# One piece of w1 and w2 under way at a time, the modulation's columns in two parts, and six attention steps ahead of the MLP

## The chip, the cores and the metric

The kernel runs on one core of a Trainium2 chip. Its time is the device time of one execution in microseconds. A core has a matrix engine (TensorE, PE in the profile), three engines for elementwise work (VectorE or DVE, ScalarE or ACT, GpSimd or POOL) and SyncE (SP), which here issues nearly all transfers; the transfers of all queues run on the core's 16 DMA engines. Each engine works its instructions off in the order in which they stand in the program, and waits for others by semaphores.

## The reference

The input is x of 2048 tokens with 448 columns, and everything is bfloat16. The block is an attention with a sliding dilated window and an MLP, both with a layer norm modulated by a condition c:

```python
mod = (_silu(c) @ w_mod).reshape(c.shape[0], 6, 1, -1)     # sa, ca, ga, sb, cb, gb
h = _layernorm(x) * (1 + ca) + sa
x = x + ga * A(h, wqkv, wo)      # 16 heads of 28; each token sees 8 tokens, two apart, itself and those before
h = _layernorm(x) * (1 + cb) + sb
x = x + gb * B(h, w1, b1, w2, b2)   # layer norm, gelu(y @ w1 + b1) @ w2 + b2, with 1792 inner columns
```

## The kernel before

The tokens are taken as two halves, the even and the odd ones, so that the dilated window becomes a window of 8 neighbours. There are 16 blocks of 128 tokens. The work is cut into named pieces ("items"), and a small planner (`Plan.schedule`) places them: it gives each item an engine and a start by a table of assumed durations, with a priority that is made of the length of the chain behind the item, a bias for its kind, its place in the sequence of tokens, and a correction of its own (`delta`). The program is then written out in the order of the planned starts, and the hardware keeps that order on each engine. Nothing is planned while the kernel runs.

The items in the order of the data:

- `ldwmod1` loads three pieces of w_mod (rows 0 to 255 and 320 to 447 in two, and the 64 rows from 256 in the third). `modcol` (L497 to L503) multiplies silu(c) with it, 8 columns of 4 parts each, and `mcol` makes of it the scale and shift of the first norm.
- `st`, `pw`, `nm`, `zt`, `md` are the first norm, the turning of its result (on TensorE for the first eight blocks, L559; by a DMA transpose for the others, L551) and the modulation into `hT`.
- `qk` multiplies `hT` with `Wqk`, in five chunks of tokens; `v` multiplies it with `Wv`. V goes to a DRAM buffer `vd` (`vt`, L693) and comes back as `vb` (`vl`, L759), laid out by windows. `wcp` (copies at L296 and L298) builds `Wqk` from the raw weights.
- `attention(d)` is one of nine steps of four windows each, 57 tokens per window: `lt` (logits, L726), `ex` (exponential, L736), `mk` (mask, L743), `dn` (row sums, L770), `pv` (L783), `ln` and `rc` (the reciprocal of the sums by logarithm and exponential, L793, L798), `on` (normalisation into `qT`, L807).
- `wo_pair` multiplies with wo and adds to x (L824, L833). `norm2` is the second and the third norm, on VectorE and GpSimd, and ends with a DMA transpose into `hT` (L890).
- `w1_pairs(q)` and `w2_block(b)` are the MLP of a quarter of the tokens: seven pairs of multiplications with w1 (L619 and L626 with tile `w`), gelu (L917), and four blocks of fourteen multiplications with w2 (L933), whose rows are scaled by gb beforehand (`w2s`, L1010). The last block is cut in two column parts (L940).
- `fill` are multiplications of zeros (L465), 28 of them, which the planner puts where TensorE would have nothing else at the start.

`CFG['phases']` sets the order of attention steps (E) and MLP quarters (G). ScalarE's exponentials and gelus need different tables, so the ScalarE work of a phase waits for that of the phase before; the multiplications with w1 wait for the logits of the phase before, those with w2 for nothing of the kind:

```python
CFG['phases'] = [['E', [0, 1, 2, 3, 4]], ['G', [0]], ['E', [5, 6, 7, 8]], ['G', [1, 2, 3]]]
```

The loads are items too. With `lag=n` a load waits for the landing of the load n places ahead of it. The wait is on SyncE, so all transfers that stand behind it in SyncE's order wait with it. The w1 and w2 loads (L577 to L587, four pieces each of 336 or 448 KB) have `lag=3`, and are held until the eight DMA transposes of the first norm have landed. The planner counts for a load 1.1 us from its start, its bytes at 0.36 MB per us, and a landing time; for the `vl` loads the landing time is 1.0.

Of the kernel before, what the change touches and what calls it, by code (L numbers as in the profile page):

```python
# [14 lines left out]
S, D, H, DH, F = 2048, 448, 16, 28, 1792  # L15
NB = S // 128
SL = S // 2
OFF = [0, 128, 192, 320]
# [19 lines left out]
    "nfill": 26,  # L38
    "gq": 1,
# [27 lines left out]
class Plan:  # L67
# [162 lines left out]
CFG["tail"], CFG["slope"], CFG["window"] = 0.0735, 17.2213, 0.15  # L230
CFG["bias"] = {
    "bce": (-107.09, 0.452),
    "cst": (91.44, 8.357),
    "dn": (-20.05, 0.02),
    "exp": (-542.16, 2.185),
    "gelu": (-247.7, 0.104),
    "h2": (-372.66, 40.0),
    "ln": (-71.79, 0.407),
    "lt": (349.79, 5.389),
    "md": (250.29, 14.017),  # L240
    "mk": (378.46, 0.25),
    "mod2": (-102.92, 0.065),
    "nm1": (-212.52, 0.208),
    "nm2": (420.37, 6.471),
    "on": (253.1, 18.885),
    "out": (363.15, 37.438),
    "pow1": (586.93, 0.02),
    "pow2": (49.28, 7.0),
    "pv": (-143.36, 3.574),
    "qk": (-468.53, 40.0),  # L250
    "qke": (-147.02, 0.024),
    "rc": (-599.49, 0.048),
    "st1": (-127.6, 15.441),
    "st2": (244.63, 15.735),
    "store": (143.43, 0.039),
    "v": (487.87, 3.471),
    "ve": (-355.16, 0.031),
    "vl": (-306.46, 8.681),
    "vt": (-492.77, 0.115),
    "w1": (37.08, 26.927),  # L260
    "w2": (-223.49, 40.0),
    "w2s": (-535.94, 19.732),
    "wcp": (-165.13, 0.443),
    "wo": (147.83, 14.91),
    "wos": (433.82, 16.205),
    "x1": (-329.74, 0.192),
    "xp": (-205.62, 0.972),
    "yt": (-95.58, 0.094),
    "zt": (-495.74, 2.221),
    "ztp": (-35.54, 0.05),  # L270
}
CFG['phases'] = [['E', [0, 1, 2, 3, 4]], ['G', [0]], ['E', [5, 6, 7, 8]], ['G', [1, 2, 3]]]
# [13 lines left out]
def build_plan(cfg):  # L286
    P = Plan(cfg)
    T = Names()
    add, val = P.add, P.val
# [13 lines left out]
    def psf(v):  # L303
        return T.ps[v.slot]
# [45 lines left out]
    def fn(e):  # L350
        memset(e, T.nhalf[:], -0.5)
# [9 lines left out]
    woz = add("woz", "cst", {"ACT": 1.7}, fn, rd=["zero"], wr=["woz"])  # L361
# [128 lines left out]
    def fn(e):  # L490
        copy(e, T.silu_bc[:], T.silu[:].unsqueeze(2).to_broadcast([128, 4, 32]))
    add("silubc", "mod2", {"DVE": 0.2, "ACT": 0.3}, fn, rd=["silu"], wr=["silu_bc"])

    v2 = val("ps", "modcol")

    def fn(e):
        w = wmod1()  # L497
        for g in range(8):
            vv, j = divmod(g, 4)
            for kt in range(4):  # L500
                T.nc.tensor.matmul(psf(v2)[:, g:g + 1], lhsT=w[:, kt, vv * D + OFF[j]:vv * D + OFF[j] + 128],
                                   rhs=T.silu[:, kt:kt + 1], start=(kt == 0), stop=(kt == 3))
    add("modcol", "front", {"PE": 0.9}, fn, rd=[("wmod1", 0), ("wmod1", 1), ("wmod1", 2), "wmodz", "silu"], wr=["ps_mod"], vals=[v2, fv])  # L503

    def fn(e):
        T.nc.vector.tensor_tensor(out=T.mcol[:], in0=psf(v2)[:, 0:8], in1=T.oz[:], op=ALU.add)
    add("mcol", "front", {"DVE": 0.1}, fn, rd=["ps_mod", "oz"], wr=["mcol"], vals=[v2])


    for m in range(4):  # L510
        for a in range(2):
            def fn(e, a=a, m=m):
                c0 = a * 512 + m * 128
                dst = T.Wqk[:, :, c0:c0 + 128].rearrange("p s (h e) -> p s h e", e=32)[:, :, :, 0:DH]
                c0 = a * D + m * 112
# [61 lines left out]
    for hh in range(2):  # L577
        for j in range(2):
            def fn(e, hh=hh, j=j):
                return e.dma_start(**overl(T.w1[:, :, 896 * hh:896 * hh + 896], T.w1_d, j, 896 * hh, 896 * hh + 896))  # L580
            load(f"ldw1{hh}{j}", 256 * 896 * 2, fn, [("w1", hh, j)], lag=3, hold=zts)
    W2P = [(0, 4), (4, 7), (7, 11), (11, 14)]
    for i, (f0, f1) in enumerate(W2P):
        def fn(e, f0=f0, f1=f1):
            return e.dma_start(out=T.w2[:, f0:f1, :],
                               in_=T.w2_d.rearrange("(ft p) n -> p ft n", p=128)[:, f0:f1, :])
        load(f"ldw2{i}", (f1 - f0) * 128 * 896, fn, [("w2", f) for f in range(f0, f1)], lag=3, hold=zts)  # L587
# [120 lines left out]
    def attention(d):  # L708
# [44 lines left out]
        for u in range(2):  # L753
            k0 = sub_tok(4 * d + 2 * u) - (WIN - 1)

            def fn(e, u=u, k0=k0):
                src = bass.AP(tensor=T.vd.tensor, offset=T.vd.offset + (16 + k0) * D,
                              ap=[[D, SK], [SQ * D, 2], [1, D]])
                T.nc.sync.dma_start(out=T.vb[vbv.slot][64 * u:64 * u + 64, :, 0:D], in_=src)  # L759
            add(f"vl{d}.{u}", "vl", {"SP": 0.6}, fn, rd=[("vd", b // 2) for b in blocks_of(k0, SQ + SK)] + ["ebuf", "vdz"],  # L760
                wr=[("vb", d, u)], vals=[vbv], land=(1.0, 128 * 896))
# [410 lines left out]
```

## Time and profile before

| what | value |
|---|---|
| median of 3 runs | 178.07 us (176.08 to 178.91) |
| the profiled execution | 177.01 us |
| its span | 175.3 us |
| granted TensorE clock | 0.999 |
| TensorE busy | 165.8 us, 95% of the span |
| VectorE, ScalarE, GpSimd busy | 117.6, 108.9, 38.8 us |
| read from and written to HBM | 11.87 and 3.70 MB |

The profile is one execution, seen by the hardware's profiler. A row of a group gives the line, the engine, the operation, what it writes and reads, how many there were, and then the busy time, the mean duration in ns, and the idle time of the engine just before, with what ended it. "issue" stands for an idle time that nothing in the profile ended. In the timeline a row begins with its start and its duration in us. The rows of stages give for each stretch the time, then busy time and number of instructions for PE, PEld (the weight loads of TensorE), DVE, ACT and POOL, the granted clock, the share of the DMA engines that was busy and the rate.

### The profile page before, as it was taken

How to read it: one execution, taken by the hardware profiler on the slowest of the kernel's cores; microseconds unless marked ns; L12 is line 12 of the kernel's file. 1: busy time of each engine (PE TensorE's matmuls, PEld its weight loads, DVE VectorE, ACT ScalarE, POOL GpSimd, SP SyncE). 2: the span in 40 equal slices, each digit the busy share in tenths (PEclk: the TensorE clock that was granted, in tenths of full speed). 3: DMA queues.
4: the chain of work that ended last, by engine and by line, in shares of the span. 5: the costliest groups of instructions: out<-in, count | busy, mean ns of one | idle time of the engine just before them, and what ended most of it. 6: DMA issues, size and time to landing. Idle time of an engine off the chain costs nothing.

```text
span 175.3 us, 5204 instructions
## 1 busy us (share of the span) xinstructions
PE 165.8 (95%) x2163; PEld 82.0 (47%) x2163; DVE 117.6 (67%) x324; ACT 108.9 (62%) x203; POOL 38.8 (22%) x63
## 2 busy tenths in 40 slices
PE   7999989999769999999998999999999999999993
PEld 2556536445335444434565554345344444445562
DVE  3679979967967999898795979999982101102121
ACT  3878995897957668876977799460090571471000
POOL 7213030601321511011242041113313202102000
PEclk9999999999999999999999999999999999999999
DMA  5999598555999913103032030034032020000311
GB/s 172 358 363 309 192 257 196 115 94 145 354 323 262 197 34 77 36 0 60 7 61 56 4 103 9 0 65 61 0 60 52 21 95 0 0 0 0 108 52 52
DMA packets 28622, 19.06 MB, mean 109 GB/s; under 512 B 14229, under 2 KB 28598, under 8 KB 28598
## 3 DMA queue, kind: packets, MB, share of 16 engines
q1 hardware_dynamic: 28182, 18.27, 38.1%
q10 hardware_dynamic: 416, 0.46, 0.8%
q8 instruction: 17, 0.28, 0.6%
q14 instruction: 7, 0.06, 0.1%
HBM read 11.87 MB, written 3.70 MB: 89 GB/s over the span
## 4 chain that ended last, share of the span: by engine, by line
PE 79%; DMA 11%; DVE 4%; SPq 3%; issue 2%; DVEq 0%
PE ps L619 35%; PE ps L933 21%; PE ps L626 7%; PE ps L824 7%; DMA hm<-in_w_mod_dram 5%; DMA x_all<-in_A_x_dram 3%; PE ps L783 3%; PE ps L726 3%; DMA vb<-vd 2%; PE ps L940 2%; PE ps L770 1%; DVE et L743 1%; DVE qT L807 1%; SPq L448 1%; DVE st L851 1%
## 5 line engine op out<-in xcount | busy, mean ns | idle before, releaser
L917 ACT ACTIVATE hm<-ps,b1c 128x512 bf16<-128x512 f32 x56 | 34.1, 693 | 29.3 <-PE ps L626 26.5
L933 PE MATMUL ps<-w,hm 128*128 128x448 bf16 x210 | 41.9, 353 | 0.0
L619 PE MATMUL ps<-hT,w 128*128 128x512 bf16 x168 | 38.6, 379 | 0.0
L950 DVE TENSOR_TENSOR x_all<-ps,xp 128x448 bf16<-128x448 f32 (+2 forms) x17 | 10.1, 595 | 34.0 <-PE ps L933 32.0
L933 PEld LDWEIGHTS <-hm 128*128 128x128 bf16 x210 | 20.1, 98 | 19.3 <-issue 0.8
L845 POOL TENSOR_TENSOR xp<-x_all,gbb 128x448 f32<-128x448 bf16 x16 | 17.2, 1078 | 43.0 <-DVE x_all L950 29.0
L619 PEld LDWEIGHTS <-w 128*128 128x128 bf16 x168 | 15.9, 98 | 21.1 <-issue 3.3
L859 POOL TENSOR_TENSOR rs<-tv,nhalf 128x2 f32<-128x2 f32 x16 | 12.2, 760 | 55.1 <-DVE tv L854 54.6
L619 PE MATMUL ps<-hT,Wqk 128*128 128x512 bf16 (+1 forms) x120 | 23.0, 337 | 0.0
L736 ACT ACTIVATE et<-ps 128x464 bf16<-128x464 f32 x36 | 17.5, 574 | 5.1 <-PE ps L726 5.1
L807 DVE TENSOR_TENSOR qT<-ps,rec 128x456 bf16<-128x456 f32 x18 | 11.4, 631 | 8.4 <-PE ps L824 3.0
L619 PEld LDWEIGHTS <-Wqk 128*128 128x128 bf16 x120 | 10.9, 98 | 9.2 <-issue 2.1
L824 PE MATMUL ps<-wo,qT 128*128 128x448 bf16 x64 | 14.3, 354 | 0.0
L743 DVE TENSOR_TENSOR et<-et,mask 128x928 bf16<-128x928 bf16 x18 | 13.3, 764 | 0.5 <-ACT et L736 0.4
L296 ACT CAST kT<-ps 128x512 bf16<-128x512 f32 x16 | 9.5, 592 | 5.1 <-PE ps L626 4.1
L296 ACT CAST qT<-ps 128x512 bf16<-128x512 f32 x16 | 9.4, 592 | 3.8 <-DVE qT L807 2.6
L833 DVE TENSOR_TENSOR x_all<-ps,x_all 128x448 bf16<-128x448 f32 x16 | 9.8, 618 | 1.9 <-PE ps L824 1.7
L532 POOL TENSOR_TENSOR rs<-tv,nhalf 128x2 f32<-128x2 f32 x8 | 5.8, 728 | 23.1 <-DVE tv L528 22.7
L619 PE MATMUL ps<-Wv,hT 128*128 128x448 bf16 x48 | 10.3, 353 | 0.0
L525 DVE BATCH_NORM_STATS2 st<-x_all 128x6 f32<-128x448 bf16 x16 | 9.2, 614 | 1.6 <-DMA x_all<-in_A_x_dram 1.6
L793 ACT ACTIVATE rec<-ps 128x464 f32<-128x464 f32 x18 | 9.7, 591 | 0.9 <-PE ps L770 0.9
L783 PE MATMUL ps<-et,vb 64*32 64x58 bf16 x576 | 6.8, 192 | 3.5 <-issue 2.7
(91 smaller groups left out, 193.8 us busy)
## 6 DMA issues: line engine op xcount, KB each, us to landing
w<-in_B_w_dram SPq DMA_DIRECT2D x6, 448.0 KB, 5.5
hm<-in_w_mod_dram SPq DMA_DIRECT2D x5, 448.0 KB, 4.6
vb<-vd SPq DMA_DIRECT2D x18, 112.0 KB, 3.4
vd<-hm SPq DMA_DIRECT2D x8, 224.0 KB, 5.5
x_all<-in_A_x_dram SPq DMA_DIRECT2D x3, 448.0 KB, 5.9
out_dram<-x_all SPq DMA_DIRECT2D x3, 448.0 KB
hm<-in_A_wqkv_dram SPq DMA_DIRECT2D x2, 448.0 KB
w<-in_B_w_dram SPq DMA_DIRECT2D x2, 336.0 KB, 4.7
```

The lines of the kernel that those rows point to most:

```text
L296: T.nc.scalar.copy(out=out, in_=in_)
L619: nc.tensor.matmul(outs[o], lhsT=stat(o, sl, 0, 128), rhs=mov(o, sl, 0, 128), start=(i == 0 and not flip and o // 2 % nb == 0), stop=(i == ...
L626: nc.tensor.matmul(outs[o], lhsT=stat(o, sl, lo, lo + 64), rhs=mov(o, sl, lo, lo + 64), start=(flip and o // 2 % nb == 0), stop=(not flip ...
L736: T.nc.scalar.activation(out=T.et[ev.slot][:, r * 464:(r + 1) * 464], in_=psf(lv[r])[:, 0:464], func=ACT.Exp, scale=float(DH) ** -0.5)
L743: T.eng[e].tensor_tensor(out=t, in0=t, in1=T.mask[:], op=ALU.mult)
L783: T.nc.tensor.matmul(psf(po[u])[32 * r:32 * r + 32, P_ * 232 + m * SC:P_ * 232 + (m + 1) * SC], lhsT=T.vb[vbv.slot][64 * u:64 * u + 64, P_ ...
L807: T.nc.vector.tensor_tensor(out=T.q[:, :, c0:c0 + 2 * SQ].rearrange("p m (a c) -> p m a c", a=2), in0=v4(psf(po[u])[:, 0:464]), in1=v4(T.r ...
L824: T.nc.tensor.matmul(psf(vs[a])[:, 0:D], lhsT=T.q[:, m, c0:c0 + 128], rhs=T.wo[:, m, :], start=(m == 0), stop=(m == 3))
L845: T.eng[e].tensor_tensor(out=T.xp[xpv[b].slot][:], in0=T.x[:, b, :], in1=T.gbb2[:], op=ALU.add)
L859: T.nc.gpsimd.tensor_tensor(out=T.rs2[i][:, bs[0]:bs[0] + 2], in0=T.tv2[i][:, bs[0]:bs[0] + 2], in1=T.nhalf[:, 0:2], op=ALU.pow)
L917: T.nc.scalar.activation(out=T.hm[hmv[q].slot][:, 512 * f:512 * f + 512], in_=psf(v)[:, 0:512], func=ACT.Gelu_apprx_tanh, bias=T.b1c[:, f: ...
L933: T.nc.tensor.matmul(psf(v)[:, 0:D], lhsT=T.hm[hmv[q].slot][:, 512 * f + 128 * (b % 4):512 * f + 128 * (b % 4) + 128], rhs=T.w2[:, f, :], ...
```

## The change

Four places of the code change, and the planner's weights with them.

- The loads of w1 and w2 get `lag=cfg["wlag"]`, which is 1: each waits for the landing of the one ahead of it.
- `modcol` becomes two items. The first takes the parts 0, 1 and 3 of all eight columns and needs the first two pieces of w_mod; the second takes part 2, and needs the 64-row piece. The 32 multiplications are the same in number and size.
- The phases become six steps, a quarter of the MLP, three steps, and three quarters.
- The planner counts 1.5 us instead of 1.0 for the landing of a `vl` load.
- All biases, corrections and the other weights of the planner are replaced, so the order of all items is drawn anew.

```diff
     "nfill": 26,
+    "wlag": 1,
...
-CFG["tail"], CFG["slope"], CFG["window"] = 0.0735, 17.2213, 0.15
+CFG["tail"], CFG["slope"], CFG["window"] = 1.7945, 17.6328, 0.0
 CFG["bias"] = {
-    "bce": (-107.09, 0.452),
...
+    "bce": (-221.91, 1.551),
...
-CFG['phases'] = [['E', [0, 1, 2, 3, 4]], ['G', [0]], ['E', [5, 6, 7, 8]], ['G', [1, 2, 3]]]
+CFG['phases'] = [['E', [0, 1, 2, 3, 4, 5]], ['G', [0]], ['E', [6, 7, 8]], ['G', [1, 2, 3]]]
...
-CFG['hold'] = 0.08
-CFG['margin'] = 39.0
+CFG['hold'] = 0.03
+CFG['margin'] = 13.0
...
-    def fn(e):
-        w = wmod1()
-        for g in range(8):
-            vv, j = divmod(g, 4)
-            for kt in range(4):
-                T.nc.tensor.matmul(psf(v2)[:, g:g + 1], lhsT=w[:, kt, vv * D + OFF[j]:vv * D + OFF[j] + 128],
-                                   rhs=T.silu[:, kt:kt + 1], start=(kt == 0), stop=(kt == 3))
-    add("modcol", "front", {"PE": 0.9}, fn, rd=[("wmod1", 0), ("wmod1", 1), ("wmod1", 2), "wmodz", "silu"], wr=["ps_mod"], vals=[v2, fv])
+    for part, kts in enumerate(((0, 1, 3), (2,))):
+        def fn(e, part=part, kts=kts):
+            w = wmod1()
+            for kt in kts:
+                for g in range(8):
+                    vv, j = divmod(g, 4)
+                    T.nc.tensor.matmul(psf(v2)[:, g:g + 1], lhsT=w[:, kt, vv * D + OFF[j]:vv * D + OFF[j] + 128],
+                                       rhs=T.silu[:, kt:kt + 1], start=(kt == 0 and g == 0), stop=(kt == 2 and g == 7))
+        add(f"modcol{part}", "front", {"PE": (0.68, 0.24)[part]}, fn,
+            rd=([("wmod1", 2), "wmodz"] if part else [("wmod1", 0), ("wmod1", 1)]) + ["silu"] + (["ps_mod0"] if part else []),
+            wr=["ps_mod" if part else "ps_mod0"], vals=[v2, fv])
...
-            load(f"ldw1{hh}{j}", 256 * 896 * 2, fn, [("w1", hh, j)], lag=3, hold=zts)
+            load(f"ldw1{hh}{j}", 256 * 896 * 2, fn, [("w1", hh, j)], lag=cfg["wlag"], hold=zts)
...
-        load(f"ldw2{i}", (f1 - f0) * 128 * 896, fn, [("w2", f) for f in range(f0, f1)], lag=3, hold=zts)
+        load(f"ldw2{i}", (f1 - f0) * 128 * 896, fn, [("w2", f) for f in range(f0, f1)], lag=cfg["wlag"], hold=zts)
...
-                wr=[("vb", d, u)], vals=[vbv], land=(1.0, 128 * 896))
+                wr=[("vb", d, u)], vals=[vbv], land=(1.5, 128 * 896))
```

More of the change, by code (lines that the diff above doesn't have):

```diff
@@ new lines @@
+    "bce": (-221.91, 1.551),
+    "cst": (279.18, 2.628),
+    "dn": (-190.34, 0.02),
+    "exp": (-526.95, 1.57),
+    "gelu": (-480.19, 11.069),
+    "h2": (-286.3, 40.0),
+    "ln": (279.25, 26.859),
+    "lt": (147.13, 0.031),
+    "md": (-471.73, 0.02),
+    "mk": (387.98, 0.024),
+    "mod2": (-39.52, 7.572),
+    "nm1": (541.87, 2.289),
+    "nm2": (122.27, 0.246),
+    "on": (38.65, 0.305),
+    "out": (-61.95, 0.298),
+    "pow1": (-331.11, 0.143),
+    "pow2": (-403.1, 0.059),
+    "pv": (-198.93, 0.027),
@@ new lines @@
+    "qk": (-120.68, 40.0),
+    "qke": (-150.08, 1.774),
+    "rc": (72.45, 1.499),
+    "st1": (220.72, 14.004),
+    "st2": (233.44, 31.607),
+    "store": (318.63, 27.719),
+    "v": (-99.59, 0.04),
+    "ve": (-236.36, 0.26),
+    "vl": (-598.91, 4.393),
+    "vt": (-473.27, 0.79),
+    "w1": (-393.26, 4.088),
+    "w2": (-22.12, 0.69),
+    "w2s": (296.09, 40.0),
+    "wcp": (-413.32, 2.652),
+    "wo": (-337.04, 0.857),
+    "wos": (356.65, 0.083),
+    "x1": (171.77, 0.042),
+    "xp": (302.77, 20.04),
@@ L271 @@
+    "yt": (434.88, 1.139),
+    "zt": (-570.12, 2.035),
+    "ztp": (464.4, 0.717),
 }
-CFG['phases'] = [['E', [0, 1, 2, 3, 4]], ['G', [0]], ['E', [5, 6, 7, 8]], ['G', [1, 2, 3]]]
+CFG['phases'] = [['E', [0, 1, 2, 3, 4, 5]], ['G', [0]], ['E', [6, 7, 8]], ['G', [1, 2, 3]]]
 CFG['gq'] = 1
@@ L282 @@
+CFG['hold'] = 0.03
+CFG['margin'] = 13.0
+CFG['pen'] = {'bce': -0.32, 'front': -0.23, 'md': 1.21, 'mod2': 0.03, 'qke': 0.35, 've': 0.55, 'wcp': -0.31}
 class Names:
```

41 lines of the change are left out of this document (1 added, 40 removed).

## The prediction

> **What bounds the kernel now.** I read the page first, for the shares and the slices, then what TensorE waited for, then the seconds around its longest wait on TensorE and on SyncE, and last the busy times by stage.
>
> ```profile
> span 175.3 us, 5204 instructions
> PE 165.8 (95%) x2163; PEld 82.0 (47%) x2163; DVE 117.6 (67%) x324; ACT 108.9 (62%) x203; POOL 38.8 (22%) x63
> ...
> PE   7999989999769999999998999999999999999993
> ...
> DVE  3679979967967999898795979999982101102121
> ...
> DMA  5999598555999913103032030034032020000311
> ...
> q1 hardware_dynamic: 28182, 18.27, 38.1%
> ...
> q8 instruction: 17, 0.28, 0.6%
> ```
>
> TensorE is busy for 165.8 of 175.3 us and is the bound; VectorE is nearly as full up to about two thirds of the span and then nearly idle. So only three things move the end: time in which TensorE stands still, filler multiplications that real work could replace, and a new wait that an engine before it (VectorE, or a queue of transfers) hands to it. The profiled execution took 177.01 us, 1.7 more than its span, and the median of the runs is 178.07. All sums below start from 177.0.
>
> ```profile
> PE ps L783 <- issue: 2.7, 1, 2.7
> ...
> PE ps L726 <- DVE qT L807: 1.0, 2, 0.8
> PE ps L783 <- DMA vb<-vd: 0.9, 1, 0.9
> ```
>
> One wait is by far the longest, 2.7 us, and nothing that the profile knows released it. This is the place:
>
> ```profile
> 46.71 0.39 PE L770 MATMUL ps<-et,one 64*32 64x232 bf16 x16
> 46.92 0.23 PE L783 MATMUL ps<-et,vb 64*32 64x58 bf16 x15
> 49.83 0.55 PE L783 MATMUL ps<-et,vb 64*32 64x58 bf16 x49 [2.67 <-issue]
> ```
>
> TensorE stops after 15 of the 64 multiplications of one PV step, whose operands were all there, and goes on with the other 49. A semaphore can't do that in the middle of a step. What can is a lack of instructions: the page has 17 instruction packets for 2163 + 2163 TensorE instructions, about 254 to a packet of some 16 KB, and they come over the same 16 DMA engines as the data.
>
> ```profile
> core 0: us, PE busy (x) PEld busy (x) DVE busy (x) ACT busy (x) POOL busy (x), PEclk, DMA share, GB/s
> 9.00:17.00 8.00, 8.00 (x123) 4.81 (x122) 6.99 (x26) 6.56 (x14) 2.17 (x3) 1.00 1.02 331
> ...
> 42.30:46.90 4.60, 4.60 (x161) 2.57 (x168) 4.47 (x13) 4.04 (x10) 2.21 (x2) 1.00 0.95 299
> 46.90:50.40 3.50, 0.83 (x81) 0.65 (x66) 2.87 (x9) 3.50 (x8) 0.51 (x1) 1.00 1.05 372
> 57.00:70.00 13.00, 13.00 (x204) 5.76 (x202) 12.60 (x39) 9.31 (x20) 3.78 (x5) 1.00 0.49 100
> 80.00:94.00 14.00, 13.97 (x343) 7.74 (x341) 10.74 (x25) 11.15 (x22) 4.49 (x5) 1.00 0.25 55
> 94.00:105.00 11.00, 9.71 (x320) 5.83 (x320) 8.61 (x18) 8.70 (x19) 2.34 (x3) 1.00 0.14 46
> ```
>
> In the 4.6 us ahead of the stop TensorE used 161 + 168 = 329 instructions, more than a packet, while the DMA engines were 0.95 to 1.05 busy. From 80 to 105 it used instructions as fast or faster (684 in 14 us, 640 in 11 us) at a DMA share of 0.25 and 0.14, and lost 0.03 and 1.3 us, no stop of that kind. So I read the 2.7 us as a block of instructions that came late behind the pieces of w1 and w2.
>
> **One piece of w1 and w2 under way.** Now SyncE issues three pieces at once and waits only from the fourth on:
>
> ```profile
> 41.14 1.61 SPq L580 DMA_DIRECT2D w<-in_B_w_dram  x3
> 42.85 1.09 SPq L693 DMA_DIRECT2D vd<-hm  x2
> 45.15 0.37 SPq L580 DMA_DIRECT2D w<-in_B_w_dram  x1
> 46.30 3.58 SPq L585 DMA_DIRECT2D w<-in_B_w_dram  x2
> 49.92 0.48 SPq L693 DMA_DIRECT2D vd<-hm  x1
> 50.53 1.26 SPq L759 DMA_DIRECT2D vb<-vd  x2
> ...
> SPq L585 <- DMA w<-in_B_w_dram: 3.5, 2, 2.8
> ...
> SPq L580 <- DMA w<-in_B_w_dram: 1.1, 1, 1.1
> ```
>
> No piece runs alone in this trace, so its time is bounded. The fourth piece goes out when the first has landed, 45.15 - 41.14 = 4.0 us with two more behind it; the other end is a 112 KB transfer:
>
> ```profile
> DMA to landing us min/median/max: 3.1/3.4/5.1
> ...
> L1010 DVE TENSOR_TENSOR w<-w,gb 128x448 bf16<-128x448 bf16 x14 | 4.4, 383 | 0.0
> ...
> 70.36 5.29 PE ps L619 x24
> ...
> 81.79 1.32 PE ps L933 x7
> ```
>
> (The first row is that of the vb transfers, L759.) A 448 KB piece alone takes between 3.1 and 4.0 us; I take 4.0, since its size is that of the upper row. Eight in a chain from 41.1 end at about 73 us, the four of w1 at about 57. The first use of w1 is near 70 and that of the last rows of w2 near 82, with 14 scalings of 0.38 us on VectorE ahead of it, of which only the last piece's three (1.1 us) can be late. Cover is 13 us for w1 and 8 us for w2, so the stretching itself costs nothing; without that cover, each microsecond of lateness would be one of TensorE's. The DMA share in 41 to 57 falls from nearly full to well under it, because between two pieces there is a landing and an issue. With that the late block goes: **-2.7** (bounds: 0 if the block comes late all the same, and -2.7).
>
> The price lies in the queue. SyncE issues in order, and seven pieces now wait for the piece ahead, where three waits took 3.5 + 1.1 = 4.6 us. Behind a waiting piece stand the vd stores, the vb loads that PV needs and the transposes of z and y. The planner puts a piece at 1.1 us of start, 1.27 of bytes and 0.9 of landing, 3.3 in all; if it takes 4.0, each wait holds SyncE for 0.7 us more than the order was laid out for. Bounds are nothing (another engine's wait covers it) and 7 x 0.7 = 4.9 us. A vb load is issued several microseconds ahead of its PV as a rule, so I take **+0.5**.
>
> **The landing time of vb, 1.5 instead of 1.0 in the plan.** It adds no instruction; it makes the order ask for a vb load 0.5 us earlier or place its PV later. The only row it answers to is the 0.9 us wait for vb above. Bounds 0 and -0.9, I take **-0.5**.
>
> **Columns of the modulation in two parts.** The 32 multiplications stay 32; 24 of them no longer wait for the 64-row piece of w_mod.
>
> ```profile
> 5.84 0.20 PE L501 MATMUL ps<-silu,hm 128*128 128x1 bf16 x2 [0.17 <-DMA hm<-in_w_mod_dram]
> 6.28 0.89 PE L501 MATMUL ps<-silu,hm 128*128 128x1 bf16 x30 [0.23 <-DMA hm<-in_w_mod_dram]
> ...
> 9.90 2.43 ACT L296 COPY Wqk<-hm 128x448 bf16<-128x448 bf16 x5 [1.32 <-DMA hm<-in_A_wqkv_dram]
> ...
> 10.51 0.60 PE L465 MATMUL ps<-zero 128*128 128x512 bf16 x2
> ```
>
> The multiplications lost 0.2 us to the load and then took 0.89 for 30. Half of those could be done by 6.28, so the columns end up to 0.4 us earlier. But the Wqk copies wait for their own load until 9.90, and TensorE does filler (0.60 us at 10.51) between V and QK. The 0.4 us become filler: **0** (bounds 0 and -0.4).
>
> **Six attention steps ahead of the MLP.** Nothing is added: the same steps, table loads and multiplications, in other places. The first stage gets a sixth step, the second has three, beside the same four W2 blocks.
>
> ```profile
> L743 DVE TENSOR_TENSOR et<-et,mask 128x928 bf16<-128x928 bf16 x18 | 13.3, 764 | 0.5 <-ACT et L736 0.4
> ...
> L807 DVE TENSOR_TENSOR qT<-ps,rec 128x456 bf16<-128x456 f32 x18 | 11.4, 631 | 8.4 <-PE ps L824 3.0
> ...
> L833 DVE TENSOR_TENSOR x_all<-ps,x_all 128x448 bf16<-128x448 f32 x16 | 9.8, 618 | 1.9 <-PE ps L824 1.7
> ```
>
> At the end of the second stage (94 to 105) TensorE lost 11.0 - 9.71 = 1.3 us: the W2 blocks were used up and step waited on step. With three steps for four blocks this gets less; bounds 0 and -1.3, I take half, **-0.6**. Against it, the sixth step brings 2 x 0.76 + 2 x 0.63 = 2.8 us of VectorE into a stage where VectorE is 12.60 of 13.00 busy. Norm work for later blocks can give way to it, so I take nothing here; its price uncovered is a rival below.
>
> **The order drawn anew.** All priorities change, so every step may sit elsewhere. TensorE's idle time in the body is 175.3 less 165.8, less about 1.3 of start and 2.9 of end, 5.3 us; without the 2.7 it is 2.6. A new order may lose it all or have it twice: bounds -2.6 and +2.6, I take 0.
>
> **Sum:** 177.0 - 2.7 + 0.5 - 0.5 - 0.6 = **173.7 us**. Against the median of 178.07 that is 2.5% less. About 2% (3.6 us) is what a measurement of this kernel can tell from no change, given runs between 176.08 and 178.91: faster is below 174.5, slower above 181.6. I hold 173.7 for the median too, since a late block of instructions is a thing that would vary from run to run, and what the median has above the profiled run may go with it.
>
> **Rivals.**
>
> *The queue is what counts (slower).* SyncE, held by seven waits, sends vb loads and transposes late, and TensorE waits for them in its own order. For it: one such wait lasted 2.8 us, and vb loads issued at 50.53 stood right behind. Against it: only 0.9 us of waiting for vb is in the whole trace, with three such waits. If each of seven lasts 2.8 us, SyncE stands for 19.6 us instead of 4.6; with half of the 15 us hidden by loads issued early, 7.5 us reach TensorE: 177.0 - 2.7 + 7.5 = 181.8, and without the gain of the late block more. It decides once a wait is over 1.5 us, today's mean. I put it at 182. [...]
>
> *The stop stays.* If the late block has nothing to do with the number of pieces, only the small terms are left: 177.0 + 0.5 - 0.5 - 0.6 = 176.4. For it: from 9 to 17 us the DMA engines are as full (1.02) and TensorE never stops. Against it: there it uses 245 instructions in 8 us, less than half the pace ahead of the stop. [...]
>
> *VectorE takes the sixth step badly (slower).* In 57 to 70 it is 97% busy, so its share of a sixth step pushes the first MLP part back by what doesn't give way. At the least that is the masks, the normalisations and two additions of 0.62, 2.8 + 1.2 = 4.0 us; at the most a ninth of all its work, 117.6 / 9 = 13.1. Half way is 8.5: 177.0 - 2.7 - 0.5 + 8.5 = 182.3, and with the 4.0 it is 177.8. Against it: VectorE's digits are 9 up to 130 us and near 1 after, so norm work has where to go.
>
> **Chances.** The forecast has 0.58, with a range of its own of 171.5 to 175.5, and 0.53 of it lies below 174.5. The queue has 0.19, all slower. The stop that stays has 0.12, of which 0.10 within 2% and 0.02 faster. VectorE has 0.11: 0.07 slower, 0.04 within. Together: faster 0.53 + 0.02 = 0.55; within 2% 0.05 + 0.10 + 0.04 = 0.19; slower 0.19 + 0.07 = 0.26. The range is 170.0 (the forecast with the lower bounds of vb, of the second stage and of part of the new order) to 183.0 (the queue case with a microsecond over).
>
> **What would show it.** Right: no stop of 2 us inside a PV step; the pieces of w1 and w2 apart on SyncE by 3.1 to 4.0 us, with a DMA share clearly under 0.9 from 41 on; w1 used after it landed without a wait; TensorE idle under 4 us in the body; less than 1.3 us lost at the end of the second stage. Wrong: TensorE waiting for vb, for hT or for w by more than 2 us in sum (the queue); a stop with "issue" as its cause, as long as now (the stop stays); VectorE at 97% with TensorE waiting for et or qT ahead of the first MLP part (the sixth step). A total above 175.5 would say that the order drawn anew has costs that no row here shows.

## The result, and the profile after

The changed kernel is slower. Its median over four runs is 181.66 us (180.46 to 182.35), beside 177.07 us (175.61 to 178.91) for the kernel before in the same rounds; the ratio is 1.029, with a 95% interval of 1.024 to 1.035. The profiled execution took 182.03 us where that of before took 177.01. (Each ratio here leaves disturbed runs out, so it can lie a little off that of the two medians.)

The page of the changed kernel:

```profile
span 180.3 us, 5198 instructions
...
PE 168.8 (94%) x2163; PEld 82.7 (46%) x2163; DVE 116.9 (65%) x322; ACT 111.1 (62%) x205; POOL 39.9 (22%) x63
...
PE   7999999799965999999999988999999999999993
...
PEclk9999999999999699999999999999999999999999
DMA  5999769668757965642003360003142000002011
```

The amount of work is the same, 2163 multiplications. TensorE is busy for 3.0 us more and idle for 2.0 us more (180.3 - 168.8 = 11.5 beside 9.5). One place stands out: the twelfth and thirteenth slice, where TensorE drops to 6 and 5 tenths, and the fourteenth, where its granted clock drops to 6 tenths. The DMA digits did fall, as forecast: from the eighth slice on only one is a 9, where the kernel before had four in a row. That one is again the fourteenth. What TensorE waited for, longest first (line waiting, releaser: us in total, times, longest):

```profile
PE ps L787 <- issue: 2.3, 1, 2.3
PE ps L787 <- DVE et L747: 1.8, 3, 1.2
...
PE ps L828 <- DVE qT L811: 1.1, 2, 0.6
PE ps L828 <- ACT kT L297: 0.8, 1, 0.8
```

The wait that nothing released is still at the head, 2.3 us where it was 2.7. (Lines lie 4 higher than in the kernel before: L787 is PV, L828 is wo.) No wait for `vb` and none for `hT<-y` is in the list. Instead there are three small groups of waits of an attention step for the step ahead of it (`et`, `qT`, `kT`), 3.7 us together. TensorE's timeline around the stop:

```profile
55.89 0.59 PE L787 MATMUL ps<-et,vb 64*32 64x58 bf16 x43
58.80 0.34 PE L787 MATMUL ps<-et,vb 64*32 64x58 bf16 x21 [2.32 <-issue]
59.07 3.00 PE L828 MATMUL ps<-wo,qT 128*128 128x448 bf16 x8
...
77.94 1.46 PE L623 MATMUL ps<-hT,w 128*128 128x512 bf16 x6
```

It is the same picture as before: a PV step cut in two, 43 of its 64 multiplications ahead of the stop and 21 behind. What is new is the row behind it, 8 multiplications in 3.00 us. The last row is the first multiplication with w1; nothing is noted that it waited for. SyncE's timeline for the same time:

```profile
44.23 0.46 SPq L584 DMA_DIRECT2D w<-in_B_w_dram  x1
44.79 1.81 SPq L763 DMA_DIRECT2D vb<-vd  x2
48.24 4.44 SPq L584 DMA_DIRECT2D w<-in_B_w_dram  x2
52.73 0.46 SPq L697 DMA_DIRECT2D vd<-hm  x1
53.86 0.58 SPq L763 DMA_DIRECT2D vb<-vd  x1
56.34 0.37 SPq L584 DMA_DIRECT2D w<-in_B_w_dram  x1
...
73.07 0.38 SPq L589 DMA_DIRECT2D w<-in_B_w_dram  x1
```

The pieces of w1 go out at 44.23, 48.24, 52.30 (the second of the pair that ends at 52.68) and 56.34, about 4.0 us apart: one under way at a time, as the change says. But from 44 to 60 there is no time without one: the stop, from 56.48 to 58.80, begins just as the third has landed and the fourth goes out. Stages of the changed kernel, in the columns of the stages before:

```profile
core 0: us, PE busy (x) PEld busy (x) DVE busy (x) ACT busy (x) POOL busy (x), PEclk, DMA share, GB/s
51.00:56.40 5.40, 3.83 (x150) 2.14 (x149) 5.32 (x16) 4.68 (x11) 1.02 (x1) 1.00 0.59 153
56.40:58.90 2.50, 0.18 (x29) 0.10 (x21) 1.23 (x3) 1.45 (x4) 0.00 (x0) 0.89 0.62 157
58.90:62.40 3.50, 3.50 (x32) 1.51 (x31) 1.62 (x4) 1.60 (x3) 0.92 (x1) 0.59 1.06 175
...
94.00:105.00 11.00, 11.00 (x312) 6.21 (x309) 10.53 (x26) 8.99 (x20) 5.69 (x5) 1.00 0.34 39
105.00:111.00 6.00, 4.87 (x130) 2.69 (x128) 3.12 (x7) 4.04 (x6) 1.04 (x1) 1.00 0.37 102
```

In the stop the DMA engines are at 0.62, where they were full in the stop before; the block was late all the same. After it TensorE is busy for 3.50 of 3.50 us, but at a granted clock of 0.59. In the last two rows the loss at the end of the second stage is not gone: it moved from before 105 us to after, 1.13 us beside 1.29.

### The profile page after: what moved, and what is told of

It reads as the page before. It is cut to its first block, busy times and chain, and to the rows that moved or that the text cites. A ratio compares the mean times of both kernels' runs of the same rounds, so it can differ in the third digit from the quotient of the medians.

```text
span 180.3 us, 5198 instructions
## 1 busy us (share of the span) xinstructions
PE 168.8 (94%) x2163; PEld 82.7 (46%) x2163; DVE 116.9 (65%) x322; ACT 111.1 (62%) x205; POOL 39.9 (22%) x63
## 4 chain that ended last, share of the span: by engine, by line
PE 79%; ACT 9%; DVE 4%; DMA 4%; issue 2%; SPq 1%; POOL 0%; DVEq 0%; ACTq 0%
PE ps L623 30%; PE ps L937 22%; PE ps L828 7%; PE ps L630 6%; PE ps L466 4%; ACT hT L595 4%; PE ps L787 3%; DMA hT<-z 2%; PE ps L730 2%; ACT et L740 2%; PE ps L944 1%; DMA vb<-vd 1%; DVE et L747 1%; PE ps L774 1%; ACT kT L297 1%
## 5 line engine op out<-in xcount | busy, mean ns | idle before, releaser
L937 PE MATMUL ps<-w,hm 128*128 128x448 bf16 x210 | 40.9, 353 | 0.0
L863 POOL TENSOR_TENSOR rs<-tv,nhalf 128x2 f32<-128x2 f32 x16 | 12.9, 807 | 49.8 <-DVE tv L858 49.4
L740 ACT ACTIVATE et<-ps 128x464 bf16<-128x464 f32 x36 | 18.4, 594 | 2.6 <-PE ps L730 2.6
L828 PE MATMUL ps<-wo,qT 128*128 128x448 bf16 x64 | 15.4, 378 | 2.2 <-DVE qT L811 1.1
L747 DVE TENSOR_TENSOR et<-et,mask 128x928 bf16<-128x928 bf16 x18 | 10.9, 631 | 1.7 <-ACT et L740 1.7
L297 ACT CAST kT<-ps 128x512 bf16<-128x512 f32 x14 | 8.4, 598 | 5.6 <-PE ps L630 4.0
L536 POOL TENSOR_TENSOR rs<-tv,nhalf 128x2 f32<-128x2 f32 x8 | 6.0, 747 | 25.6 <-DVE tv L532 25.1
L787 PE MATMUL ps<-et,vb 64*32 64x58 bf16 x576 | 7.2, 193 | 4.1 <-issue 2.3
L802 ACT ACTIVATE rec<-rec 128x464 f32<-128x464 f32 x18 | 10.6, 599 | 0.5
L466 PE MATMUL ps<-zero 128*128 128x512 bf16 x28 | 9.4, 487 | 1.3 <-DVE oz L302 1.3
```

What stands on the lines that cost most here:

```text
L466: T.nc.tensor.matmul(psf(fvl)[:, 0:512], lhsT=T.zero[:, 0:128], rhs=T.zero[:], start=True, stop=True)
L740: T.nc.scalar.activation(out=T.et[ev.slot][:, r * 464:(r + 1) * 464], in_=psf(lv[r])[:, 0:464], func=ACT.Exp, scale=float(DH) ** -0.5)
L747: T.eng[e].tensor_tensor(out=t, in0=t, in1=T.mask[:], op=ALU.mult)
L787: T.nc.tensor.matmul(psf(po[u])[32 * r:32 * r + 32, P_ * 232 + m * SC:P_ * 232 + (m + 1) * SC], lhsT=T.vb[vbv.slot][64 * u:64 * u + 64, P_ ...
L828: T.nc.tensor.matmul(psf(vs[a])[:, 0:D], lhsT=T.q[:, m, c0:c0 + 128], rhs=T.wo[:, m, :], start=(m == 0), stop=(m == 3))
L863: T.nc.gpsimd.tensor_tensor(out=T.rs2[i][:, bs[0]:bs[0] + 2], in0=T.tv2[i][:, bs[0]:bs[0] + 2], in1=T.nhalf[:, 0:2], op=ALU.pow)
```

## The experiments

Two theories stood at the beginning. **The stop theory**: the order of the change holds the time, and one piece at a time neither cures the stop nor costs much. **The waits theory**: SyncE, held by seven waits, delays what stands behind them. After the first runs a third came up, that **the six steps** cost by themselves. Ratios are to the kernel before in the same rounds.

### The waits alone, from both sides

The changed kernel with the waits of the kernel before, all else as in the change:

```diff
+        waits = [loads[-3]] if name.startswith(("ldw1", "ldw2")) else after
...
-            for a in after:
+            for a in waits:
```

> The changed kernel, every item in its place, but the w1 and w2 loads wait again for the piece three places ahead instead of the one ahead. If the queue is what costs (SyncE held by seven waits), the loads behind it come earlier and the time falls by 3 us or more, to about 178. If the loss is in the new order and in the late block of instructions, the time stays within 1 us of 181.7 and the stop inside a PV step stays at 2 us or gets longer, since three pieces are under way again.

Measured: 178.88 us (178.06 to 179.37), ratio 1.014 (1.004 to 1.023); span 177.6, clock 1.00. Its TensorE timeline at the same place (lines lie one higher again, L788 and L829):

```profile
56.96 0.27 PE L788 MATMUL ps<-et,vb 64*32 64x58 bf16 x21 [0.75 <-issue]
57.17 1.89 PE L829 MATMUL ps<-wo,qT 128*128 128x448 bf16 x8
```

With up to three pieces under way the stop is 0.75 us, not 2.32, and the same 8 multiplications behind it take 1.89 us, not 3.00. The loads lie elsewhere, too: here the first three have gone out by 47.41, and the fourth follows at 54.22. The two differences, 1.57 and 1.11, make 2.7 us, which is the difference of the spans. So the waits cost 180.3 - 177.6 = 2.7 us, about 1.6% of the 2.9%, and they cost it at the very place where they were to help.

The other side is the kernel before with waits one place ahead (a lag of 1 written out in the same way) and the order as it was:

> The kernel before, every item in its place, with nothing changed but the waits: each w1 and w2 load waits for the one ahead of it. If one piece under way lets the block of instructions through, the stop of 2.7 us falls to under 1 and the time to about 175. If a single piece holds it as well, the stop stays and the time is 177. If the held queue costs, PV waits for vb or the transposes of y come late: 179 or more.

Measured: 189.2 us (187.49 to 190.06), ratio 1.071 (1.060 to 1.083). Its waits on TensorE and SyncE, then its SyncE timeline and its PV step where it matters (L627 is the second half of the w1 pairs, L581 and L586 are the loads of w1 and w2, L891 the transposes of y):

```profile
PE ps L627 <- DMA hT<-y: 8.9, 1, 8.9
...
SPq L586 <- DMA w<-in_B_w_dram: 10.5, 4, 3.5
...
SPq L581 <- DMA w<-in_B_w_dram: 8.1, 3, 3.1
```

```profile
67.74 0.38 SPq L586 DMA_DIRECT2D w<-in_B_w_dram  x1
...
69.37 2.56 SPq L891 DMA_TRANSPOSE hT<-y  x2
...
73.54 2.54 SPq L891 DMA_TRANSPOSE hT<-y  x2
```

```profile
47.37 0.73 PE L784 MATMUL ps<-et,vb 64*32 64x58 bf16 x64
```

SyncE stands for 18.6 us, and the transposes that the first w1 multiplication needs stand behind the loads of w2, at 69.4 to 76. TensorE waits 8.9 us for them in one piece, and its granted clock is low there and behind it: 0.66 from 70 to 80 us, which holds the end of the wait, 0.88 from 80 to 94, and 0.972 over the whole span. PV has no stop at all here: in this order one piece at a time does cure it. So the queue rival was right in mechanism, and the victim that counts is `hT<-y` and not `vb`, for which TensorE waits 0.7 us in sum. In the changed kernel that wait is absent, because its order was laid out with the waits in it. Waits two places ahead, in the order before:

> The kernel before, every item in its place, with waits two places ahead for the w1 and w2 loads, halfway between three (before) and one. If the held queue costs in proportion, the y transposes end a few us later: with one place they were 9 us too late for the first w1, and with three they had about 8 us to spare, so with two the last piece goes out near 58 us and nothing waits; the stop shrinks to 0.5 to 1.5: 174.5 to 176. If TensorE waits for hT by more than 1 us: 177 to 180.

Measured: 176.74 us, ratio 1.000 (0.995 to 1.005). The stop falls to 0.49 us, and a wait of 1.26 us ahead of the first w1 pair takes its place.

### What the stop needs

No waits at all between the loads, order before (`waits = []` for all eight), one run:

> The kernel before, every item in its place, with no waits between the w1 and w2 loads, so that up to eight pieces are under way. If a block of instructions stands behind the pieces, the stop in the PV step near 47 us grows from 2.7 to 4 us or more and the time to 178 or more. If a block waits for a packet only, the stop doesn't grow: 2.7 or less, and 175 to 177.

Measured: 177.82 us. The stop in its timeline:

```profile
50.68 0.55 PE L784 MATMUL ps<-et,vb 64*32 64x58 bf16 x49 [2.79 <-issue]
```

With all eight free to be under way it is 2.79 us, where it was 2.67 with three, 0.49 with two and nothing with one. So in the traces of this order the stop grows with the number of pieces up to three, and not beyond.

The traces show what comes just ahead of the end of the stop, for they hold the times of the instruction packets too (queue q8, 17 packets of 16,384 bytes each). In the kernel before, one runs from 47.37 to 48.25, and TensorE goes on at 49.83; in the changed kernel one runs from 56.39 to 57.36, and TensorE goes on at 58.80. In all five traces above with a stop, TensorE goes on 1.4 to 1.6 us after such a packet has ended. With one piece at a time in the order before, the packet runs from 45.09 to 45.99 already, ahead of the PV step at 47.37. So I read the stop as a block of instructions that comes late.

How late it comes can be counted from TensorE's own instructions. A packet holds about 254 of them by the prediction's estimate (4326 instructions over 17 packets), so I take the 254 (multiplications and weight loads) ahead of the stop. The kernel before begins them at 42.73 and the last of them 4.2 us later; the changed kernel begins them at 53.22 and the last 3.1 us later. Counted from the first of them, the packet began 4.6 us later in the kernel before, with three pieces just gone out, about 2.3 us later with two and 2.1 us with one; in the changed kernel 3.2 us later, with one piece out since 52.30. When a block is asked for, no trace shows. By this count the packet runs earlier with fewer pieces in the order before; in the changed kernel it ran 1.1 us later than there with one piece, and TensorE had gone through the instructions ahead of it in 1.1 us less than the kernel before.

Next, all loads of w1 and w2 moved away from PV, in both orders. In the order of before they go behind the last `vl` ahead of the first transposes of y; in that of the change (waits three ahead) behind the first of these transposes:

```diff
     order = P.schedule()
+    wl = [it for it in order if it.name.startswith(("ldw1", "ldw2"))]
+    order = [it for it in order if it not in wl]
+    at = [it.name for it in order].index("yt0") + 1      # order before: index("vl5.0") + 1
+    order[at:at] = wl
```

> The kernel before, but all w1 and w2 loads stand behind the last vb load of that stretch on SyncE, just ahead of the first transposes of y, some 10 us later and behind the place of the stop. If the block of instructions is late because of these pieces, the stop goes and the time is 174 to 174.8. If not, it stays at 177. If the loads are now late for the MLP, TensorE waits for w near 70 us and the time is above 178.

> The changed kernel, every other item in its place, but all w1 and w2 loads stand behind the first two transposes of y on SyncE (some 10 us later, behind the place of the stop) and wait three places ahead. If the late block of instructions comes from these pieces, the stop of 2.3 us shrinks to 0.7 or less and the low clock after it goes: about 178 to 178.5. If the block is late for another reason, stop and time stay (181 to 182). If w1 or w2 now come too late, TensorE waits for w near 80 us and the time is above 182.

Measured: 179.64 us, ratio 1.018 (1.005 to 1.031), in the order before; 180.79 us, ratio 1.026 (1.014 to 1.037), in the order after. The stop is gone in both (0.1 us at most), so it does hang on a load beside it. But the transposes of y are late in both, by 2.5 and 1.7 us. In the first, the stage of that wait and the one behind it:

```profile
core 0: us, PE busy (x) PEld busy (x) DVE busy (x) ACT busy (x) POOL busy (x), PEclk, DMA share, GB/s
67.90:70.60 2.70, 0.16 (x4) 0.11 (x4) 2.05 (x6) 2.20 (x5) 0.00 (x0) 1.00 0.69 78
70.60:75.00 4.40, 4.40 (x15) 1.51 (x15) 4.40 (x14) 1.43 (x2) 0.00 (x0) 0.61 0.20 52
```

Again a pause of some 2.5 us, and then a clock of 0.61. The pause is paid twice. So a smaller move, in the order before: the first three pieces of w1 only, and only behind the next two `vd` stores, some 2 us later.

```diff
+    wl = [it for it in order if it.name in ("ldw100", "ldw101", "ldw110")]
+    order = [it for it in order if it not in wl]
+    at = [it.name for it in order].index("vt5") + 1
+    order[at:at] = wl
```

> The kernel before, every item in its place, but the first three w1 pieces stand behind the two vd stores that followed them on SyncE, about 2 us later, still with waits three places ahead. If the stop of 2.7 us comes from a block of instructions asked for at about 42.6 us that stands behind these three pieces, the block now gets ahead of them: no stop, the transposes of y move by at most 2 us and stay covered, time 173.5 to 174.5 against about 176.5. If the block is late whenever the pieces follow closely, the stop stays at 2 us or moves to the next block: 176 to 177.

Measured: 175.54 us over ten runs (174.59 to 176.51) beside 176.63 over nineteen, ratio 0.993 (0.990 to 0.997); span 174.8. Its SyncE and TensorE timelines:

```profile
43.38 1.59 SPq L693 DMA_DIRECT2D vd<-hm  x2
45.02 5.33 SPq L580 DMA_DIRECT2D w<-in_B_w_dram  x4
```

```profile
48.98 0.73 PE L783 MATMUL ps<-et,vb 64*32 64x58 bf16 x64
```

PV runs through, 64 in one row of 0.73 us. The loads are still three at a time, the DMA engines nearly as loaded (0.92 from 45 to 49 us), and the wait is gone. Of the 2.7 us, 1.1 us of median arrive at the end. In the profiled execution the PV step begins at 48.98, where it began at 46.92, so there about 2.1 us were lost ahead of it; 1.2 us of them are a wait for a piece of w_mod, which the edit doesn't move. Whether other executions lose them too is not shown. The same kind of move in the order after, with its waits one ahead, takes the last two pieces of w1 behind the second half of the `vb` of step 4 (`vl4.1`):

```diff
+    wl = [it for it in order if it.name in ("ldw110", "ldw111")]
+    order = [it for it in order if it not in wl]
+    at = [it.name for it in order].index("vl4.1") + 1
+    order[at:at] = wl
```

> The changed kernel with its one-at-a-time waits, every item in its place, but the third and the fourth w1 piece stand behind the vd store and the vb loads that followed them on SyncE, so that no piece goes out between 48.3 and about 54 us. If what the waits cost is the stop and the low clock behind it (a single piece in flight when the block of instructions is asked for at about 53 us), stop and clock drop go and the time falls by 2.5 to 3.5 us to 178 to 179. If what costs is SyncE being held, the chain of pieces ends as late as before or later and the time stays above 180.5.

Measured: 185.32 us, ratio 1.041 (1.032 to 1.049).

```profile
PE ps L623 <- DMA hT<-y: 6.2, 1, 6.2
...
PE ps L787 <- issue: 0.3, 1, 0.3
```

The stop goes, and the queue takes its place: each later piece now waits in front of the transposes. In each of the three kernels with one at a time, either the stop stays or the transposes are late.

### The six steps

What is left, 1.4% with the old waits, is the order with its six steps. ScalarE is busy for 111.1 us in the changed kernel beside 108.9 before, and TensorE waits for its `kT`; so one version put modulation work on VectorE, in the changed kernel with the old waits: `it.eng = "DVE"` for `md1.1`, `md2.1`, `md3.1` and those of `md8` and `md12`.

> The changed kernel with waits three places ahead, every item in its place, but eight modulations that its plan gave to ScalarE run on VectorE, as they do in the kernel before (three of the six halves for blocks 2 to 7, and those for blocks 8 to 15). If ScalarE, full from 17 to 30 us and waiting for hT transposes after, is what costs the changed order its 2.5 us, the second logits come 1 us or more earlier and the time falls by 1 to 2 us from 178.9. If VectorE's order is as tight, the time stays within 0.7 us.

Measured: 180.25 us, ratio 1.022 (1.015 to 1.028), where 1.014 stood without it: no gain. If ScalarE is too full there, giving this work to VectorE doesn't help. Then the phases alone: the kernel before, its weights, waits and code, planned with 6-1-3-3.

```diff
-CFG['phases'] = [['E', [0, 1, 2, 3, 4]], ['G', [0]], ['E', [5, 6, 7, 8]], ['G', [1, 2, 3]]]
+CFG['phases'] = [['E', [0, 1, 2, 3, 4, 5]], ['G', [0]], ['E', [6, 7, 8]], ['G', [1, 2, 3]]]
```

> The kernel before with its own weights, waits, modulation and landing times, but planned with six attention steps, a quarter of the MLP and three steps. The order is the same up to the fifth step's logits (about 61 us). If the six steps pay at the end of the second stage as predicted, the time is 0 to 1 us below before. If the sixth step's chain holds the first MLP quarter, the time is 2 to 5 us above before, with TensorE waiting for et, qT or a free bank between 65 and 85 us.

> The kernel before, planned with six, one, three and three parts of the phases (as in the run that came out 2.5% slower), and with the three w1 pieces behind the two vd stores, so that the stop in the PV step goes. If the six steps cost by themselves (a PV, an output multiplication and a bank waited for between 77 and 82 us, and the table loads behind them), the time stays 1.5% or more above before, 179 or more. If most of that run's loss was the stop and the low clock behind it, the time is within 1% of before, 176 to 178.

Measured: 182.82 us (180.67 to 185.03), ratio 1.025 (1.014 to 1.035) for the phases alone. The second is the same with the three pieces moved as above, so that no stop is in it: 179.49 us (178.94 to 180.16), ratio 1.019 (1.015 to 1.023), span 177.2. Beside the 0.993 of the move alone this is 2.6%, some 4.5 us, for the six steps by themselves under the old weights; the two medians lie 4.0 us apart and the two spans 2.4. Where they lie, in the stages of 52 to 97 us, first of the kernel with the move alone, in two parts, then with six steps:

```profile
core 0: us, PE busy (x) PEld busy (x) DVE busy (x) ACT busy (x) POOL busy (x), PEclk, DMA share, GB/s
52.00:82.00 30.00, 29.58 (x359) 13.26 (x360) 27.74 (x79) 22.57 (x42) 7.16 (x9) 1.00 0.60 139
82.00:97.00 15.00, 14.22 (x406) 8.15 (x403) 11.06 (x22) 12.55 (x25) 4.08 (x4) 1.00 0.16 36
```

```profile
52.00:97.00 45.00, 41.68 (x820) 20.27 (x824) 37.07 (x97) 34.12 (x65) 9.62 (x11) 1.00 0.42 89
```

TensorE is idle for 0.42 + 0.78 = 1.2 us in the first and for 45.00 - 41.68 = 3.3 us in the second. Its timeline with six steps, and ScalarE's at the same place:

```profile
72.69 0.92 PE L824 MATMUL ps<-wo,qT 128*128 128x448 bf16 x4 [0.67 <-ACT rec L793]
...
74.94 0.66 PE L783 MATMUL ps<-et,vb 64*32 64x58 bf16 x63 [1.21 <-DVE x_all L833]
...
76.09 1.46 PE L619 MATMUL ps<-hT,Wqk 128*128 128x512 bf16 x5 [0.49 <-ACT hm L917]
```

```profile
72.08 1.01 ACT L793 ACTIVATE rec<-ps 128x464 f32<-128x464 f32 x2 [3.05 <-PE ps L770]
...
74.06 1.28 ACT L917 ACT_TABLE_LOAD   x1
```

At the turn from the sixth step to the MLP, wo waits for the reciprocal, the last PV for an addition on VectorE to free its place, and the multiplications behind for the first gelu, which itself follows a table load of 1.28 us: 2.4 us in 5. ScalarE had been idle for 3.05 us just before, so it is not short of time but late in a chain: sums, reciprocal, normalisation, wo, addition. That accounts for 2.1 of the 2.4 us by which the spans differ; the medians differ by more, and the rest isn't placed.

### The modulation's columns, and versions that might win

The columns' parts in the order 0, 1, 3, 2 in the kernel before, as one item:

```diff
-        for g in range(8):
-            vv, j = divmod(g, 4)
-            for kt in range(4):
+        for kt in (0, 1, 3, 2):
+            for g in range(8):
+                vv, j = divmod(g, 4)
...
-                                   rhs=T.silu[:, kt:kt + 1], start=(kt == 0), stop=(kt == 3))
+                                   rhs=T.silu[:, kt:kt + 1], start=(kt == 0 and g == 0), stop=(kt == 2 and g == 7))
```

> The kernel before, every item in its place, with the columns of the modulation in the changed order: three parts of all eight columns first, the part with the 64-row piece last. If this is hidden behind the Wqk load as predicted, the time is that of before within 0.5 us. If the front counts, up to 0.4 us less.

Measured: 176.06 us, ratio 0.997 (0.994 to 1.001): nothing that can be told. Together with the moved pieces:

> The kernel before with the two edits that did no harm: the three w1 pieces behind the two vd stores, and the columns of the modulation with the 64-row piece last. If the column order is worth the 0.3% that its own run showed (within its error), the time is 174.8 to 175.3, 0.7 to 1.1% below before; if it is nothing, 175.5, as the shifted kernel.

Measured: 175.44 us over twelve runs (174.08 to 177.55), ratio 0.994 (0.990 to 0.998). It can't be told from the move alone; both beat the kernel before and the changed one. A third version added two moves on TensorE to the shifted pieces, `m2` behind `v2` and `pv0` behind `qk1.0`, to fill two waits of about 1 us at the start:

> The kernel before with the three w1 pieces behind the two vd stores (as in the run that was 0.7% faster), and two TensorE steps moved by one place: the row form of the modulation behind the third V, the first PV behind the next QK, because TensorE stood before them for 0.4 to 1.2 us and 0.5 to 1.4 us in the runs so far. If these waits are on the path to the end, another 0.8 to 1.5 us go: 173.8 to 174.7. If the work behind them takes the delay over, the time is that of the shifted kernel, 175.5, or above.

Measured: 176.81 us, ratio 1.003 (1.000 to 1.006). The two waits went, and two others of 1.0 and 0.7 us came ahead of QK and of the logits: the gain of the shifted pieces was given back.

## Why the prediction was wrong, step by step

The forecast was 173.7 us, and the direction was wrong: the time is 181.66, on the slower side, to which only the queue and VectorE were to lead.

**What bounds the kernel** was read rightly. TensorE set the end in every run, and each difference above was found as idle time or lowered clock on it.

**The stop, -2.7.** This is the step that failed first: the stop went from 2.67 to 2.32 us, so the term measured -0.35. It was read as a block of instructions late beside the loads, and the runs bear that out: moving the loads away removes it (0.1 us at most, and 64 PV multiplications in one row), and TensorE goes on 1.4 to 1.6 us after an instruction packet. (That a semaphore can't stop a step in its middle was the author's argument, and it doesn't hold for every step: the modulation's, in the kernel before, waited 0.23 us for its load after 2 of 32 multiplications. For the stop the trace names no releaser.) That the packet runs earlier with fewer pieces under way is borne out too, in the order before, where one at a time leaves no stop. What failed is to carry this over to a new order: the prediction took it that one piece lets the block through in time anywhere. Spread one by one, the pieces leave no moment without one from 44 to 60 us, and at the place of the stop the changed kernel goes through the 254 instructions ahead of it in 3.1 us where the kernel before took 4.2. A support was misread as well: the stretches from 80 to 105 us are not as fast as the one ahead of the stop. They use 684 instructions in 14 us and 640 in 11, which is 49 and 58 per us, beside 329 in 4.6, which is 72. The prediction's own bound "0 if the block comes late all the same" was the value to take, and the rival of the stop that stays had the outcome of this one step right, for another reason. How a block is held up isn't settled: the traces show when an instruction packet runs, not when it was asked for.

**A cost that no term had** is the clock behind the stop, 1.1 us on the eight wo multiplications. The kernel before had a longer stop and kept its clock in the profiled execution. Six of the 22 runs of it beside the column order have a mean clock of 0.988 to 0.990; they left no trace, so whether the stop lowered it there is open.

**The queue, +0.5.** No direct wait came, so the size was about right for this order, and a piece alone took 4.0 us, the value taken. SyncE's waits came to 11.9 us:

```profile
SPq L584 <- DMA w<-in_B_w_dram: 7.1, 3, 3.6
...
SPq L589 <- DMA w<-in_B_w_dram: 4.8, 3, 2.6
```

The rival's price was 7.5 us; in the order before it is real, and more (8.9 us of waiting, and the low clock behind it), but the order of the change was drawn with the waits in it, and there they reach TensorE only by way of the stop. The last piece went out at 73.07, where the chain was put to end at about 73, and the first w1 multiplication began at 77.94 without a wait: the cover for the stretching held.

**The landing of vb, -0.5.** The wait for `vb` is gone after, but it is gone too when only three pieces are moved, with the plan's 1.0. Under the old weights, 1.5 draws the identical order. So the 0.9 us can't be put down to this edit.

**The columns, 0.** Right.

**Six steps, -0.6.** The gain did not come: it was costed where the second stage ends, and the loss there stayed (1.13 beside 1.29 us). Under the old weights six steps even cost 2.5% (1.9% with the three pieces moved), for the most part at the other end, the turn into the MLP, by a chain and not by VectorE's share. There the rival for the sixth step had the place and the sign, with VectorE as the engine; VectorE is busy for 37.07 of 45 us, not full, with TensorE waiting for ScalarE and VectorE in turn. In the changed kernel this turn costs next to nothing: TensorE waits 0.20 us there, at 77.19, and with the old waits

```profile
74.53 0.92 PE L829 MATMUL ps<-wo,qT 128*128 128x448 bf16 x4 [0.27 <-ACT qT L297]
```

So under the new weights this price is nearly gone, and what the new order costs lies elsewhere.

**The order, 0.** This is the step that failed by most. Between 33.6 and 108 us the changed kernel with the old waits is idle for 5.1 us on TensorE, and the shifted one for 2.0 in the like stretch up to its own w1 multiplications of the second quarter:

```profile
33.60:108.00 74.40, 69.33 (x1433) 34.16 (x1433) 64.30 (x167) 61.82 (x115) 19.19 (x20) 1.00 0.47 119
33.60:57.00 23.40, 20.13 (x495) 9.78 (x497) 18.70 (x46) 20.85 (x41) 5.46 (x6) 1.00 0.63 178
```

```profile
33.60:103.60 70.00, 68.04 (x1394) 34.33 (x1402) 60.27 (x153) 57.51 (x113) 18.19 (x20) 1.00 0.47 114
```

Most of it, 23.40 - 20.13 = 3.3 us, is lost by 57 us, well ahead of the turn: 0.75 in the stop, and 2.5 where attention steps wait on one another (`kT` 0.8, `et` 1.5, `hT` 0.3). The shifted kernel has no such wait between 30 and 62 us. TensorE is also busy for 1.5 us more (167.3 beside 165.8), of which 0.6 are filler (9.4 beside 8.8). The planner's own plan, by its assumed durations, ends at 169.1 us for the order before and at 170.5 for the changed one, so it promised no gain either. What the new weights would cost with five steps is open: no run has them.

**The sum as measured**, in profiled executions: 177.0 - 0.35 for the shorter stop, + 1.1 for the clock, leaves 4.2 us of order and steps to reach 182.0. The changed kernel with the old waits gives the same 4.2: its span is 2.3 us over that of before, though its stop is 1.9 us shorter. Of the 8.3 us between forecast and profiled execution, 2.35 are the stop, 1.1 the clock, and 4.8 the order and the steps, for which -0.6 stood in the sum. The six steps by themselves under the old weights cost about as much (4.0 to 4.5 us by the medians), but at another place, so the two can't be set equal.

## What to carry to other kernels

Before transfers are spaced out to keep something else on time, ask when that is asked for, what has gone out just ahead of it, and how long it can be waited for; here moving three loads by 2 us removed the stop and gained 0.7%, and spacing eight of them removed it only where the transposes then paid. A wait on SyncE's queue cost here what stood behind it, 8.9 us of TensorE's time in the order before with one load at a time: name the last consumer in that queue (here the transposes ahead of the MLP) and not only the next. A step moved into an earlier stage is costed at both ends of the stage, by the chain from its last result to the next stage's first, even where no engine is full. And a new order of everything is a term of its own, which can be larger than those that can be read off a profile.

## What the runs showed of the hardware

In two runs a short pause was paid twice. Around the end of pauses of 2.3 and 2.5 us (the changed kernel, and the order before with late loads) TensorE's granted clock was lowered: 0.59 over the 3.5 us behind the first, 0.61 over the 4.4 us behind the second. The clock's own record in the traces has 0.5 for 3.41 us, from 58.35 and from 71.11, and the stages agree with it: what is missing of the clock makes 2 x (2.5 x 0.11 + 3.5 x 0.41) = 3.4 us at half clock in the first and 2 x 4.4 x 0.39 = 3.4 us in the second. Of the changed kernel's four runs, the one whose clock was 1.0 was also the shortest, 180.46 us, and the three at 0.989 to 0.991 took 181.29 to 182.35.

The length of the pause doesn't decide alone. After the 2.67 us stop of the profiled kernel before the clock stayed at 1.00, and with the 2.79 us of the order before without waits its mean over the span was 0.999; in the changed kernel it was lowered at 2.32 us, with TensorE busy for only 3.83 of the 5.40 us ahead of them. What decides, no run here shows.

In the changed kernel the DMA engines were not full during the stop without a releaser in the middle of a step. It was 2.3 us at a DMA share of 0.62, with one load of 448 KB under way; in the 3.1 us ahead of it, from 53.21 to 56.29, the share was 0.92. In the kernel before the share was 1.07 during the stop. TensorE went on 1.4 to 1.6 us after an instruction packet had ended, in five traces.
